# Part of the last zero fill written from GpSimd's DMA queue by 108 rows, in a decode layer with its gradients

## The chip, the cores and the metric

The kernel runs on one core of one Trainium2 chip. The metric is the device time of one execution in microseconds. Before the change it is 814.44 us, the median of 3 runs (814.18 to 814.63).

## The reference

One decode step of a transformer block (layer norm, attention over a sliding window of a key/value cache, a bilinear gated feed-forward part) and its gradients with respect to all inputs and weights:

```
W = min(4096, max(256, Sk // 4))                      # 4096 of Sk = 32768 positions
q = (x @ wq).reshape(B, Sq, Hq, Dh)                   # 16 heads of 256, x has 448 columns
k, v = k_cache[:, :, Sk - W:], v_cache[:, :, Sk - W:] # 8 key/value heads
o = softmax(q k^T / 16) v @ wo
h  = x + A(layernorm(x), k_cache, v_cache, wq, wo)
h2 = h + ((z @ w_gate) * (z @ w_up)) @ w_down,  z = layernorm(h)
outputs: h2, and d/d(x, k_cache, v_cache, wq, wo, w_gate, w_up, w_down) of <h2, grad_out>
```

What matters here: the gradients of the two caches have the full shape (8, 32768, 256) in bf16, and only the last 4096 positions of each head are not zero. The other 28,672 positions of 8 heads and 2 caches, 234.88 MB, are zeros that the kernel has to write. Everything else is about 103 MB of loads and stores.

## The kernel before

Two queues carry the DMAs. SP (in the code `FILL`) issues the two loads of one-row vectors and the zero fills; GpSimd (`IO`) issues all other loads and stores. The DMAs of both run on the same 16 DMA engines of the core.

*The fills.* A tile `zeros` of 128 rows by 8192 bf16 (16 KB a row) is set to zero once on VectorE. For each of 8 heads and for each of the two cache gradients (`out_2` for keys, `out_3` for values) one DMA at line 62 writes the head's zero region: the region is cut into 128 parts of 7 pieces of 16 KB, and row p of `zeros` is written seven times into part p. That makes 16 DMAs of 896 pieces, 14,336 KB each. They are issued at the start, one after the other, as far as SP's queue has room.

*The forward part.* For each head, GpSimd loads windows of the key and value cache (lines 79, of 2 MB each) into slots of the tile `S`; TensorE transposes and multiplies, VectorE and ScalarE empty the results. Loads are issued when a slot comes free.

*The turn.* After the last head the output projection, the feed-forward part and its gradient run with little data: GpSimd issues the second half of `wo` (line 375), `w_gate` (line 376) and `w_up` (line 377), and its next DMA is the second load of `w_down` (line 491), which waits until VectorE has done with the tile `Rt` that held `w_up`.

*The backward part.* For each head a value window is used again (some are loaded again), the gradients of the windows are formed by outer products (line 601), emptied by ScalarE and VectorE (lines 210 and 212), and stored by GpSimd from four staging slots (line 606). Weight gradients are formed on VectorE and stored between them (line 476). GpSimd's issues stand in program order, each behind the waits of those ahead of it.

The order of GpSimd's DMAs is that of the program as scheduled; the completion counters that its DMAs increase are eight, used in turn, so that a DMA that reuses one waits for the DMA eight issues before it.

Of the kernel before, what the change touches and what calls it, by code (L numbers as in the profile page):

```python
# [16 lines left out]
G = 8  # L17
Dh = 256
W = 4096
# [3 lines left out]
Sk = 32768  # L23
# [7 lines left out]
ZW = 8192  # L31
NZ = (Sk - W) * Dh // (128 * ZW)
# [8 lines left out]
def kernel(  # L41
# [4 lines left out]
    FILL = nc.sync  # L46
    IO = nc.gpsimd
# [8 lines left out]
    FILL.dma_start(out=go_bf[:], in_=grad_out.rearrange("a b d -> (a b) d"))  # L56
    zeros = const.tile([128, ZW], bf16)
    V_.memset(zeros[:], 0.0)
    for g in range(G):
        for o in (out_2, out_3):  # L60
            reg = o[0, g, 0:Sk - W, :].rearrange("s d -> (s d)").rearrange("(p n f) -> p n f", p=128, f=ZW)
            FILL.dma_start(out=reg, in_=zeros[:].unsqueeze(1).to_broadcast([128, NZ, ZW]))


    S = const.tile([128, NS, SLOT], bf16)
# [21 lines left out]
    def flat_rows(w):  # L87
        return w.rearrange("a b -> (a b)").rearrange("(p x) -> p x", p=128)
# [251 lines left out]
    wu_sb = Rt[:, 0:NI * HF]  # L340
# [33 lines left out]
                                        op0=ALU.mult, op1=ALU.add, accum_out=d_hh[:, c:c + 1])  # L374
    IO.dma_start(out=woB, in_=wo_v[:, 16:32, :])
    IO.dma_start(out=wg_sb, in_=flat_rows(B_w_gate))
    IO.dma_start(out=wu_sb, in_=flat_rows(B_w_up))


    ao = ps.tile([1, D], f32, tag="tmp", bufs=1)  # L380
# [258 lines left out]
```

## Time and profile before

| | |
|---|---|
| median of 3 runs | 814.44 us |
| span of the profiled execution, first to last instruction | 812.7 us |
| TensorE busy | 495.5 us (61%) |
| VectorE busy | 374.0 us (46%) |
| ScalarE busy | 164.7 us (20%) |
| GpSimd busy, with its issuing of DMAs aside | 40.5 us (5%) |
| read from and written to HBM | 57.28 MB and 280.59 MB, 416 GB/s over the span |
| fills, from issue to landing, median | 148.2 us, 16 times 14,336 KB |
| stores of window gradients, from issue to landing, median | 29.3 us, 16 times 2,048 KB |
| last issue of GpSimd | 769.9 us |

How to read the profile: times are microseconds from the start of the span. The engines' shares say how long each was busy, not what the end waits for. "DMA" in the slices is the mean busy share of the core's 16 DMA engines, a digit of 9 meaning 90% or more. Beside them the profile lists three kinds of DMA queue: those fed by SP in hardware, those fed by GpSimd in software, and the fetches of instructions. The time from issue to landing of a DMA holds the time it stands in its queue behind others.

### The profile page before, as it was taken

The numbers are of one execution on the slowest core, as the hardware profiler recorded it, in microseconds if no ns is written. First come the engines' busy times: TensorE is split into PE (matmuls) and PEld (weight loads), VectorE is DVE, ScalarE is ACT, GpSimd is POOL, SyncE is SP. The second block draws the span as 40 slices with busy tenths as digits, with TensorE's granted clock in tenths as the row PEclk, the third lists the DMA queues.
The fourth block names the chain that finished last, engine by engine and source line by source line (L and its number), as shares of the span: only waits on it lengthen the run. The fifth ranks groups of instructions, "written<-read, shape, count | busy, mean of one in ns | idle before, by whom it ended". The sixth has DMA issues, their size and how long they took to land.

```text
span 812.7 us, 10923 instructions
## 1 busy us (share of the span) xinstructions
PE 495.5 (61%) x4479; PEld 289.6 (36%) x4479; DVE 374.0 (46%) x1149; ACT 164.7 (20%) x261; POOL 40.5 (5%) x75
## 2 busy tenths in 40 slices
PE   3559949999647519035497576099759674554500
PEld 3545636666223405013495432044325331210100
DVE  4128727777445306005671455366455435352500
ACT  0230101222000200001001233044435342332300
POOL 3000000000000001000000100001000001000000
PEclk9959778999678758655556555555555555555555
DMA  8999999999999999999999999999999999999994
GB/s 344 427 426 429 427 433 424 432 424 429 431 422 431 418 429 429 409 430 429 427 427 433 423 410 418 430 428 417 424 406 429 424 418 419 420 427 422 427 427 187
DMA packets 24567, 338.58 MB, mean 417 GB/s; under 512 B 1251, under 2 KB 1317, under 8 KB 4677
## 3 DMA queue, kind: packets, MB, share of 16 engines
q1 hardware_dynamic: 14596, 234.88, 68.4%
q0 software_dynamic: 9920, 103.00, 30.3%
q8 instruction: 35, 0.57, 0.3%
q14 instruction: 16, 0.12, 0.0%
HBM read 57.28 MB, written 280.59 MB: 416 GB/s over the span
## 4 chain that ended last, share of the span: by engine, by line
issue 29%; DMA 16%; PE 11%; DVE 4%; POOL 2%; ACT 1%; POOLq 0%; DVEq 0%
DMA S<-in_A_v_cache_dram 4%; DMA S<-in_A_wo_dram 4%; DMA Rt<-in_A_wq_dram 4%; DMA out_dram<-Mt 3%; PE dq_ps L452 3%; PE MT L322 2%; POOL out_dram L476 1%; DVE Rt L422 1%; POOL out_dram L606 1%; PE dh_ps L159 1%; PE d_ps L601 1%; PE tr L567 1%; PE t L412 1%; PE ao L382 1%; DVE Rt L511 1%
## 5 line engine op out<-in xcount | busy, mean ns | idle before, releaser
L601 PE MATMUL d_ps<-R,Mt 32*128 32x512 bf16 x256 | 124.4, 613 | 92.4 <-DVE S L212 91.6
L322 PE MATMUL MT<-Rt,S 128*128 128x512 bf16 x512 | 145.9, 397 | 30.7 <-DMA S<-in_A_v_cache_dram 29.8
L318 DVE TENSOR_SCALAR Rt<-S,pf 128x256 bf16<-128x256 bf16 x512 | 117.0, 281 | 56.4 <-PE MT L322 49.7
L212 DVE CAST S<-d_ps 128x512 bf16<-128x512 f32 x128 | 86.7, 688 | 55.5 <-ACT S L210 44.0
L210 ACT CAST S<-d_ps 128x512 bf16<-128x512 f32 x128 | 75.0, 586 | 169.8 <-PE d_ps L601 169.8
L601 PEld LDWEIGHTS <-Mt 32*128 32x128 bf16 x256 | 23.3, 114 | 146.1 <-issue 144.7
L567 PE MATMUL tr<-ident_bf,S 128*128 128x128 bf16 x512 | 69.6, 306 | 3.5 <-ACT Mt L210 3.5
L325 PEld LDWEIGHTS <-S 128*128 128x128 bf16 x512 | 49.4, 100 | 60.9 <-issue 9.5
L266 PE MATMUL tr<-ident_bf,S 128*128 128x128 bf16 x512 | 48.6, 253 | 36.4 <-DMA S<-in_A_k_cache_dram 32.0
L567 PEld LDWEIGHTS <-S 128*128 128x128 bf16 x512 | 49.2, 137 | 28.0 <-issue 27.8
L266 PEld LDWEIGHTS <-S 128*128 128x128 bf16 x512 | 38.1, 115 | 34.7 <-DMA S<-in_A_k_cache_dram 32.3
L325 PE MATMUL acc<-pT_all,S 128*128 128x2 bf16 x512 | 48.2, 166 | 0.0
L328 PE MATMUL acc<-pT_all,S 128*128 128x2 bf16 x512 | 47.5, 164 | 0.0
L322 PEld LDWEIGHTS <-S 128*128 128x128 bf16 x512 | 33.5, 98 | 36.7 <-DMA S<-in_A_v_cache_dram 30.7
L210 ACT COPY Rt<-tr 128x1024 bf16<-128x1024 bf16 x32 | 32.4, 1012 | 67.2 <-PE tr L266 66.9
L210 ACT COPY Mt<-tr 128x1024 bf16<-128x1024 bf16 x32 | 32.4, 1014 | 56.6 <-PE tr L567 29.5
L330 ACT COPY Mt<-MT 128x512 f32<-128x512 f32 x8 | 4.7, 585 | 192.3 <-PE MT L322 164.3
L382 PE MATMUL ao<-S,oT_bf 128*1 128x448 bf16 x32 | 9.6, 468 | 45.9 <-DMA S<-in_A_wo_dram 45.9
L212 DVE COPY Rt<-tr 128x1024 bf16<-128x1024 bf16 x32 | 22.0, 688 | 32.7 <-PE tr L266 31.8
L572 PEld LDWEIGHTS <-Mt 128*128 128x128 bf16 x512 | 20.0, 108 | 37.0 <-DVE Mt L212 14.0
L328 PEld LDWEIGHTS <-S 128*128 128x128 bf16 x512 | 30.9, 97 | 0.1
L572 PE MATMUL dp<-doT,Mt 128*128 128x2 bf16 x512 | 22.6, 168 | 12.6 <-DVE Mt L212 10.8
(182 smaller groups left out, 454.5 us busy)
## 6 DMA issues: line engine op xcount, KB each, us to landing
out_dram<-zeros SPq DMA_DIRECT2D x16, 14336.0 KB, 148.2
out_dram<-S POOLq DMA_DIRECT2D x16, 2048.0 KB, 29.3
S<-in_A_v_cache_dram POOLq DMA_DIRECT2D x11, 2048.0 KB, 36.3
S<-in_A_k_cache_dram POOLq DMA_DIRECT2D x8, 2048.0 KB, 29.0
out_dram<-Mt POOLq DMA_DIRECT2D x6, 896.0 KB, 22.2
S<-in_A_wq_dram POOLq DMA_DIRECT2D x1, 3584.0 KB, 14.8
S<-in_A_wo_dram POOLq DMA_DIRECT2D x2, 1792.0 KB, 31.8
out_dram<-Mt POOLq DMA_DIRECT2D x3, 1024.0 KB, 34.0
```

What stands on the lines that cost most here:

```text
L210: S_.copy(out=out, in_=in_)
L212: V_.tensor_copy(out=out, in_=in_)
L266: P_.transpose(tr[:, i, dh, :], Xw[:, 4 * q + i, dh * 128:(dh + 1) * 128], ident_bf[:])
L318: V_.tensor_scalar(out=pk[:, i, h, :], in0=K[:, t, :], scalar1=pf[:, t, h:h + 1], scalar2=None, op0=ALU.mult)
L322: P_.matmul(MT[:, hf, :], lhsT=Vv[:, t, hf * 128:(hf + 1) * 128], rhs=pk[:, i, :, :].rearrange("p h d -> p (h d)"), start=(t == 0), stop=( ...
L325: P_.matmul(acc[:, 2 * hf:2 * hf + 2], lhsT=Vv[:, t, hf * 128:(hf + 1) * 128], rhs=pT_all[:, g, t, :], start=(t == 0 and hf == 0), stop=(t ...
L328: P_.matmul(acc[:, 4 + dk:7 + dk:2], lhsT=K[:, t, dk * 128:(dk + 1) * 128], rhs=pT_all[:, g, t, :], start=False, stop=(t == T - 1), skip_g ...
L382: P_.matmul(ao[:], lhsT=oT_bf[:, b:b + 1], rhs=wo_b(b), start=(b == 0), stop=(b == 31))
L452: P_.matmul(dq_ps[:, 2 * h + dk:2 * h + dk + 1], lhsT=Mt[:, h // 2, hf, c0:c0 + 128], rhs=doT_f[:, 2 * h + hf:2 * h + hf + 1], start=(hf = ...
L567: P_.transpose(tr[:, i, dh, :], Vw[g][:, 4 * q + i, dh * 128:(dh + 1) * 128], ident_bf[:])
L572: P_.matmul(dp[:, 4 * q + i, :], lhsT=xt[:, i, dh, :], rhs=doT[:, 4 * g + dh:4 * g + dh + 3:2], start=(dh == 0), stop=(dh == 1))
L601: P_.matmul(d_ps[:, i, :, :].rearrange("p w d -> p (w d)"), lhsT=rows[32 * k:32 * k + 32, a, :], rhs=R[32 * k:32 * k + 32, :], start=True, ...
```

## The change

Fifteen of the sixteen fills stay as they are. The last one (head 7, `out_3`) is cut at five places. In units of pieces (16 KB) of its 896:

- pieces 0 to 639 are written by SP as before, in one DMA of 128 rows with 5 pieces each;
- the next 614,400 bytes (37.5 pieces) are written by SP in one DMA of 64 rows with one piece of 9,600 bytes each;
- then 14 KB by GpSimd, in one DMA of 7 rows with two pieces of 1 KB each;
- then 26 KB by GpSimd, in one DMA of 13 rows with two pieces of 1 KB each;
- pieces 680 to 895, 216 of them, by GpSimd, in one DMA of 108 rows with two pieces of 16 KB each.

GpSimd issues its three DMAs in the order 7 rows, 108 rows, 13 rows, directly behind its load of `w_up` in the turn and ahead of the second load of `w_down`. All bytes that were written are still written, each once.

```diff
+    def region(o, g):
+        return o[0, g, 0:Sk - W, :].rearrange("s d -> (s d)")
+
+    def fill(eng, flat, p, n, f):
+        eng.dma_start(out=flat.rearrange("(p n f) -> p n f", p=p, f=f), in_=zeros[0:p, 0:f].unsqueeze(1).to_broadcast([p, n, f]))
+
     for g in range(G):
         for o in (out_2, out_3):
-            reg = o[0, g, 0:Sk - W, :].rearrange("s d -> (s d)").rearrange("(p n f) -> p n f", p=128, f=ZW)
-            FILL.dma_start(out=reg, in_=zeros[:].unsqueeze(1).to_broadcast([128, NZ, ZW]))
+            if (g, o) != (G - 1, out_3):
+                fill(FILL, region(o, g), 128, NZ, ZW)
+    last = region(out_3, G - 1)
+    CUT = [0, 640 * ZW, 680 * ZW - 40 * 512, 680 * ZW - 26 * 512, 680 * ZW, NZ * 128 * ZW]
+    fill(FILL, last[CUT[0]:CUT[1]], 128, 5, ZW)
+    fill(FILL, last[CUT[1]:CUT[2]], 64, 1, 4800)
+
+    def fill_rest():
+        fill(IO, last[CUT[2]:CUT[3]], 7, 2, 512)
+        fill(IO, last[CUT[4]:CUT[5]], 108, 2, ZW)
+        fill(IO, last[CUT[3]:CUT[4]], 13, 2, 512)
...
     IO.dma_start(out=wg_sb, in_=flat_rows(B_w_gate))
-    IO.dma_start(out=wu_sb, in_=flat_rows(B_w_up))
+    wu_load = IO.dma_start(out=wu_sb, in_=flat_rows(B_w_up))
+    with tc.issue_after(wu_load.ins):
+        fill_rest()
```

## The prediction

> **What bounds the kernel now.** I read the page's slices and queues first, then the pool engine's timeline around the edit, then the last microseconds by windows, then the single DMA packets.
>
> From the page: the slices, and the DMA queues with packets, megabytes and share of 16 engines.
>
> ```profile
> DMA  8999999999999999999999999999999999999994
> GB/s 344 427 426 429 427 433 424 432 424 429 431 422 431 418 429 429 409 430 429 427 427 433 423 410 418 430 428 417 424 406 429 424 418 419 420 427 422 427 427 187
> DMA packets 24567, 338.58 MB, mean 417 GB/s; under 512 B 1251, under 2 KB 1317, under 8 KB 4677
> ...
> q1 hardware_dynamic: 14596, 234.88, 68.4%
> q0 software_dynamic: 9920, 103.00, 30.3%
> q8 instruction: 35, 0.57, 0.3%
> ```
>
> All 16 DMA engines are busy from the first slice to the last but one, at about 427 GB/s. Compute, the chain of waits included, only decides which bytes go when; the end is when the busiest DMA engine has moved its bytes. q1 is the zero fills that SP issues, q0 everything that GpSimd issues. The change moves bytes from q1 to q0 and adds none.
>
> The last stretch in windows; the last two columns are DMA share and GB/s.
>
> ```profile
> 780.00:790.00 10.00, 0.00 (x0) 0.00 (x0) 0.00 (x0) 0.00 (x0) 0.00 (x0) 0.50 1.02 431
> 790.00:796.00 6.00, 0.00 (x0) 0.00 (x0) 0.00 (x0) 0.00 (x0) 0.00 (x0) 0.50 0.99 421
> 796.00:800.00 4.00, 0.00 (x0) 0.00 (x0) 0.00 (x0) 0.00 (x0) 0.00 (x0) 0.50 0.85 365
> 800.00:803.00 3.00, 0.00 (x0) 0.00 (x0) 0.00 (x0) 0.00 (x0) 0.00 (x0) 0.50 0.37 158
> 803.00:805.00 2.00, 0.00 (x0) 0.00 (x0) 0.00 (x0) 0.00 (x0) 0.00 (x0) 0.50 0.21 90
> 805.00:807.00 2.00, 0.00 (x0) 0.00 (x0) 0.00 (x0) 0.00 (x0) 0.00 (x0) 0.50 0.12 49
> 807.00:809.00 2.00, 0.00 (x0) 0.00 (x0) 0.00 (x0) 0.00 (x0) 0.00 (x0) 0.50 0.06 25
> 809.00:811.10 2.10, 0.00 (x0) 0.00 (x0) 0.00 (x0) 0.00 (x0) 0.00 (x0) 0.50 0.05 23
> ```
>
> No engine computes any more. Shares of 0.21, 0.12 and 0.06 of sixteen are about 3, 2 and 1 engines: a few are late, and the last 4 us belong to one. The trace's packet records name no engine, but a packet starts 3 or 4 ns before the previous one of its engine ends, so engines can be followed. Their ends: twelve from 796.1 to 802.3 us (mean 799.9), then 804.6, 804.7, 806.7 and 811.1. The mean of all sixteen is 801.6: perfect balance would be worth 9.5 us. From 811.1 it is 1.6 us to the span's end (812.7), and 1.7 more to the median of the runs (814.44), so I carry differences at 811.1 over to 814.44.
>
> Why they are late: followed to 450 us, one engine's 16 KB fill pieces take 635 ns on average, the others' 612 to 619. The 35 fetches of q8, about 0.95 us each, go round eight engines in turn; the two that end at 804.6 and 804.7 have one of the last two fetches each. So the late four have different causes, and nothing in the trace says that they are neighbours in the engines' numbering.
>
> The turn, on the pool engine (start, duration, idle before), and the queues between 367 and 395 us.
>
> ```profile
> 320.39 0.53 POOL L376 DMA_DIRECT2D S<-in_B_w_gate_dram  x1 [52.12 <-PE acc L328]
> 321.97 1.17 POOL L375 DMA_DIRECT2D S<-in_A_wo_dram  x1 [1.04 <-PE acc L325]
> 324.32 0.54 POOL L377 DMA_DIRECT2D Rt<-in_B_w_up_dram  x1 [1.19 <-issue]
> 395.07 1.10 POOL L491 DMA_DIRECT2D Rt<-in_B_w_down_dram  x1 [70.21 <-DVE st L196]
> ```
>
> ```profile
> q1 hardware_dynamic: 750, 12.04, 100.5%
> q8 instruction: 1, 0.02, 0.2%
> ```
>
> GpSimd issues nothing for 70 us, and once the w_up load has landed (the view of the DMA issues gives 42.5 us, so 324.3 + 42.5 = 367 us) q0 is empty; the fills alone keep the engines full.
>
> **The change, part by part.**
>
> *Issues.* Three GpSimd DMAs of about 0.53 us behind w_up fall into its 70 us of idling: nothing. If that cover were gone they would delay the w_down load at L491 by 1.6 us, a fifteenth of its 25.8 us to landing. Nothing they wait for is late: the zeros are written at the start, and each later GpSimd DMA that reuses a completion counter waits for one eight issues older, as before. On SP the sixteenth fill becomes two DMAs; a fill lands 63 us or more after its issue begins, so SP's queue does not run dry.
>
> *q0.* 18 pieces alternating with the fills on one engine take 2 x 18 x 0.607 = 21.9 us, from 367 to 389, before the next user at 395. If they take longer, the w_down load is late by the rest; the DMA engines stay full meanwhile, so this alone costs nothing at the end.
>
> *Bytes per engine, the point of it.* A fill gives each engine 896 / 16 = 56 pieces. Now SP gives it 640 / 16 = 40 pieces and 4 of 9,600 bytes, together 42.34 pieces: 13.66 fewer, at 0.607 us 8.3 us less. The 216 pieces come back on q0. Spread evenly they would be 13.5 per engine and nothing would change. 108 rows do not split over 16 engines in whole rows; over 12 they do, 9 rows or 18 pieces each, and 7 + 12 + 13 = 32 brings a cursor round to where it was. Then twelve engines get 10.9 us and four get none. Short rows: two pieces of 1 KB at about 0.045 us and a few counts of 9 ns, 0.15 us. Net: twelve engines +2.75 us, four -8.1 us. No DMA of before has fewer than 16 engines, so which four is not in the trace.
>
> [...]
>
> *Reading rows that belong to others.* Every DMA of before has 128 rows (the one-row vectors aside), and sixteen engines then run side by side at 611 ns for 16 KB. With 9 rows per engine the 108-row DMA has the engines read zeros from rows that other engines' fills are reading at the same time. No row of before shows that. Lower bound: nothing, pieces at 611 ns. Upper bound: pieces of 1,208 ns occur (around 469 us, on most engines, when two pieces of one engine are in flight together), twice 611; if each of the 216 pieces takes that and holds another engine's piece up as long, 2 x 216 x 0.597 = 258 us of engine time, 16.1 us per engine. An engine at 611 ns has no slack to lend, and in a window of 22 us or more nearly all partners are reading; but part of the time the owner of a row is itself reading elsewhere. I take the half, 8 us per engine.
>
> [...]
>
> *Sum.* If the late four are the spared ones: 811.1 - 8.1 + 8 = 811.0 for the last of them, and 802.3 + 2.75 + 8 = 813.1 for the last of the twelve. The loss will not be even; 0.9 us more for that gives 814.0, 2.9 us later than 811.1: 814.44 + 2.9 = **817.3 us**.
>
> **The rivals.**
>
> *No crossing, late ones spared.* The twelve end at 802.3 + 2.75 = 805.1, the four by 803.0: 6.0 us earlier, 808.4 us. If only the last one and the one before it are among the four, 804.7 + 2.75 = 807.5 ends it: 3.6 us earlier, 810.8. For it: the packets' arithmetic above is exact. Against: it needs free reads, and four late engines of different causes as neighbours. From a loss of about 6 us per engine on, it is no gain.
>
> *Wrong four, no crossing.* The engine that ends at 811.1 gets 18 pieces: 811.1 + 2.75, so 817.2. With the crossing as well, 825.2.
>
> *It does not do what it says.* All sixteen engines take part, seven rows each and the last three: fifteen change by 14 - 13.66 pieces, 0.2 us, plus 0.15: 814.8 without crossing. If the engine with 6 pieces is the last one, 806.7 + 0.35 ends it: 810.4.
>
> **How the numbers follow.** About 1.6 us (0.2%) is what can be told from no change. Chances: crossing decides, 0.46; no crossing or little of it and the last engine spared, 0.37; wrong four without crossing, 0.07; sixteen engines, 0.05; a small crossing that cancels the gain, 0.05. Faster: 0.37 and a little from the fourth, 0.38. Same: 0.08. Slower: 0.54. The range goes from 808.0 (all balance gained) to 822.5, which leaves out the full upper bound of the crossing (802.3 + 2.75 + 16.1 = 821.1, so 824.5) and the wrong four with crossing. The likeliest case alone spans 815 to 822.5.
>
> **What would show it.** Pieces of q0 that write zeros between 367 and 390 us: twelve chains of 18 if the split is right. Their duration, and that of the fill pieces beside them: near 611 ns refutes the crossing, 800 to 1,200 proves it, with GB/s of that stretch falling from 431 to about 316 (22 us of work in 30). The last windows: shares falling from 1 to 0 within 3 us mean balance; a lone engine after 811 means the wrong four. The prediction is wrong if the stretch stays at 425 GB/s and the last packet ends by 808.

## The result and the profile after

The changed kernel takes 819.80 us (median of 4 runs, 819.03 to 820.24) beside 814.52 us for the kernel before (4 runs): 5.3 us slower, a ratio of 1.0066 with a 95% interval of 1.0052 to 1.0081. The profiled execution has a span of 818.3 us. The prediction put it at 817.3 us, 2.9 us above the kernel before; the direction was right, the size a little over half of the measured one.

The page of the changed kernel, the same rows as before:

```profile
DMA  8999999999999999999999999999999999999995
GB/s 344 430 424 429 425 430 429 426 428 430 426 426 430 419 425 412 425 426 332 399 430 429 409 423 416 432 421 425 421 410 425 427 416 422 422 424 424 425 427 205
DMA packets 24758, 338.58 MB, mean 414 GB/s; under 512 B 1398, under 2 KB 1464, under 8 KB 4844
...
q1 hardware_dynamic: 14420, 231.30, 67.7%
q0 software_dynamic: 10288, 106.58, 31.3%
```

The bytes are the same, 338.58 MB; 3.58 MB have gone from q1 to q0. The row of busy shares looks as before, all nines. The row of GB/s does not: the 19th slice has 332 and the 20th 399, where before there were 427 and 427. The engines were "busy" in that stretch and moved a fifth less. That is the signature of packets that take longer, not of packets that are missing.

In windows, the last two columns are DMA share and GB/s. First the turn in the kernel before:

```profile
360.00:396.00 36.00, 15.47 (x151) 9.89 (x148) 22.23 (x64) 3.75 (x7) 0.93 (x1) 0.55 1.01 430
```

Then the changed kernel, the turn and the end:

```profile
367.00:390.00 23.00, 8.43 (x120) 4.83 (x119) 17.32 (x40) 3.49 (x6) 0.00 (x0) 0.50 1.00 335
390.00:420.00 30.00, 25.69 (x118) 25.37 (x119) 21.62 (x82) 0.53 (x1) 1.15 (x1) 0.50 1.00 412
...
800.00:803.00 3.00, 0.00 (x0) 0.00 (x0) 0.00 (x0) 0.00 (x0) 0.00 (x0) 0.50 1.05 402
803.00:805.00 2.00, 0.00 (x0) 0.00 (x0) 0.00 (x0) 0.00 (x0) 0.00 (x0) 0.50 0.95 314
805.00:807.00 2.00, 0.00 (x0) 0.00 (x0) 0.00 (x0) 0.00 (x0) 0.00 (x0) 0.50 0.90 258
807.00:809.00 2.00, 0.00 (x0) 0.00 (x0) 0.00 (x0) 0.00 (x0) 0.00 (x0) 0.50 0.61 184
809.00:811.00 2.00, 0.00 (x0) 0.00 (x0) 0.00 (x0) 0.00 (x0) 0.00 (x0) 0.50 0.41 140
811.00:813.00 2.00, 0.00 (x0) 0.00 (x0) 0.00 (x0) 0.00 (x0) 0.00 (x0) 0.50 0.25 100
813.00:815.00 2.00, 0.00 (x0) 0.00 (x0) 0.00 (x0) 0.00 (x0) 0.00 (x0) 0.50 0.09 34
815.00:817.00 2.00, 0.00 (x0) 0.00 (x0) 0.00 (x0) 0.00 (x0) 0.00 (x0) 0.50 0.05 19
```

Two things stand here. In the turn the DMA engines moved 335 GB/s at a share of 1.00. And between 803 and 807 us, while SP's last DMA (64 rows of 9,600 bytes, from 802.0 us on) is written, they are busy at 0.95 and 0.90 and move 314 and 258 GB/s: a second place where they are slow, which the prediction does not have.

GpSimd's issues in the turn (start, duration, idle before):

```profile
323.38 0.54 POOL L392 DMA_DIRECT2D Rt<-in_B_w_up_dram  x1 [1.19 <-issue]
324.00 1.99 POOL L63 DMA_DIRECT2D out_dram<-zeros  x3
392.04 1.15 POOL L508 DMA_DIRECT2D Rt<-in_B_w_down_dram  x1 [66.05 <-DVE st L211]
```

The three added DMAs cost 1.99 us of issuing, and 66 us of idling lie behind them. The w_down load goes out at 392.04 (before: 395.07). The instructions of TensorE, VectorE and ScalarE, and GpSimd's other DMAs, stand in the same order as before, and GpSimd's last issue is at 768.3 us (before: 769.9). So nothing of the loss is a late computation.

The packet records give the rest; followed as in the prediction, from each packet to the next one of its engine:

```
                                    before            after
pieces of 16 KB in the turn, q1     mean 612 ns       mean 810 ns, 54% within 5% of 611, longest 1,785
pieces of 16 KB in the turn, q0     (none)            mean 740 ns, 55% within 5% of 611, longest 1,888
time above 611 ns, all of them      -                 83 us in all, 5.2 us per engine
64 pieces of 9,600 bytes at the end (none)            361 ns alone; nearly half of them 700 to 1,449 ns
ends of the 16 engines              796.1 to 811.1    804.4 to 816.8
mean of the ends                    801.6             809.9
```

The mean end is 8.3 us later at equal bytes, and the last engine ends 5.7 us later.

### The profile page after: what moved, and what is told of

Read it like the earlier page. It is cut to its first block, busy times and chain, and to the rows that moved or that the text cites. A ratio compares the mean times of both kernels' runs of the same rounds, so it can differ in the third digit from the quotient of the medians.

```text
span 818.3 us, 10895 instructions
## 1 busy us (share of the span) xinstructions
PE 493.4 (60%) x4445; PEld 289.5 (35%) x4479; DVE 374.6 (46%) x1149; ACT 164.7 (20%) x261; POOL 42.4 (5%) x78
## 2 busy tenths in 40 slices
DMA packets 24758, 338.58 MB, mean 414 GB/s; under 512 B 1398, under 2 KB 1464, under 8 KB 4844
## 4 chain that ended last, share of the span: by engine, by line
issue 26%; DMA 21%; PE 9%; DVE 4%; POOL 2%; ACT 1%; POOLq 0%; DVEq 0%
DMA out_dram<-S 5%; DMA S<-in_A_v_cache_dram 5%; DMA S<-in_A_wo_dram 4%; DMA Rt<-in_A_wq_dram 4%; DMA out_dram<-Mt 3%; PE d_ps L618 2%; PE MT L337 2%; PE tr L584 2%; POOL out_dram L493 1%; DVE Rt L439 1%; PE t L429 1%; PE ao L399 1%; POOL out_dram L623 1%; DVE Rt L528 1%; DVE S L227 0%
## 5 line engine op out<-in xcount | busy, mean ns | idle before, releaser
L337 PE MATMUL MT<-Rt,S 128*128 128x512 bf16 x478 | 139.9, 398 | 29.5 <-DMA S<-in_A_v_cache_dram 28.9
L584 PE MATMUL tr<-ident_bf,S 128*128 128x128 bf16 x512 | 69.6, 306 | 3.5 <-ACT Mt L225 3.5
L281 PE MATMUL tr<-ident_bf,S 128*128 128x128 bf16 x512 | 50.8, 260 | 33.9 <-DMA S<-in_A_k_cache_dram 28.5
```

The source lines that it names most:

```text
L281: P_.transpose(tr[:, i, dh, :], Xw[:, 4 * q + i, dh * 128:(dh + 1) * 128], ident_bf[:])
L337: P_.matmul(MT[:, hf, :], lhsT=Vv[:, t, hf * 128:(hf + 1) * 128], rhs=pk[:, i, :, :].rearrange("p h d -> p (h d)"), start=(t == 0), stop=( ...
L584: P_.transpose(tr[:, i, dh, :], Vw[g][:, 4 * q + i, dh * 128:(dh + 1) * 128], ident_bf[:])
```

## The experiments

Each edit is shown against the changed kernel. "Mean end" and "last end" are those of the sixteen engines in the profiled execution; in the kernel before they are 801.6 and 811.1. Each ratio is to the kernel before as it ran beside that kernel.

| kernel | median us | ratio to before, 95% interval | GB/s 367 to 390 | mean end | last end |
|---|---|---|---|---|---|
| changed kernel | 819.80 | 1.0066 [1.0052, 1.0081] | 335 | 809.9 | 816.8 |
| e1, 128 rows | 814.14 | 0.9998 [0.9989, 1.0008] | 432 | 802.0 | 811.0 |
| e2, 112 rows | 819.94 | 1.0066 [1.0049, 1.0083] | 342 | 808.0 | 817.3 |
| e3, SP's last DMA with 128 rows | 817.56 | 1.0040 [1.0025, 1.0055] | 343 | 808.2 | 813.9 |
| e6, e3 with the split four engines further | 823.09 | 1.0107 [1.0090, 1.0124] | 336 | 808.2 | 819.5 |
| e4, own rows, first try | 819.59 | 1.0064 [1.0049, 1.0079] | 345 | 811.5 | 815.9 |
| e5, own rows | 815.59 | 1.0008 [0.9997, 1.0020] | 431 | 806.0 | 807.3 |
| e8, e5 with GpSimd's order held | 818.10 | 1.0058 [1.0045, 1.0071] | 430 | 812.9 | 813.0 |
| e9, e8 with 12 pieces | 819.41 | 1.0055 [1.0039, 1.0070] | 428 | 815.1 | 815.1 |
| e10, e5 with every engine's order held | 810.25 | 0.9951 [0.9938, 0.9963] | 426 | 802.7 | 806.6 |
| e11, e10 with 12 pieces | 809.21 | 0.9941 [0.9927, 0.9954] | 427 | 802.0 | 805.7 |

### e1 and e2: the same move with 128 and with 112 rows

Is it the move to the other queue that costs, or the rows that are read? With 128 rows each engine was taken to read the rows that it reads in the fills; with 112 rows every engine gets seven rows, 14 pieces (976 packets of 4 bytes on q0, 61 x 16: all sixteen take part), so that no engine's bytes change, but the rows were taken to be no longer those of its fills.

```diff
-    CUT = [0, 640 * ZW, 680 * ZW - 40 * 512, 680 * ZW - 26 * 512, 680 * ZW, NZ * 128 * ZW]
+    CUT = [0, 640 * ZW, NZ * 128 * ZW]                 # e1
+    CUT = [0, 640 * ZW, 672 * ZW, NZ * 128 * ZW]       # e2
     fill(FILL, last[CUT[0]:CUT[1]], 128, 5, ZW)
-    fill(FILL, last[CUT[1]:CUT[2]], 64, 1, 4800)
+    fill(FILL, last[CUT[1]:CUT[2]], 128, 1, 2048)      # e2 alone
     def fill_rest():
-        fill(IO, last[CUT[2]:CUT[3]], 7, 2, 512)
-        fill(IO, last[CUT[4]:CUT[5]], 108, 2, ZW)
-        fill(IO, last[CUT[3]:CUT[4]], 13, 2, 512)
+        fill(IO, last[CUT[1]:CUT[2]], 128, 2, ZW)      # e1
+        fill(IO, last[CUT[2]:CUT[3]], 112, 2, ZW)      # e2
```

> 256 pieces go to GpSimd in the turn by 128 rows with two pieces each; SP writes the other 640 by 128 rows. Every engine gets what it had before, and no row is read by another engine than before. Crossing theory (engines lose time when they read rows that other engines' fills read): no loss, GB/s between 367 and 390 us stays at 425 to 431, time as before within 1 us (814.5). Rival, that fills from GpSimd's queue in the turn are themselves slow or delay the turn: 335 GB/s there as in the changed kernel, and 818 to 821 us.

> 224 pieces go to GpSimd in the turn by 112 rows with two pieces each, which 16 engines share evenly, seven rows or 14 pieces each; SP writes the rest by 128 rows. No engine gets more or less bytes than before. Crossing theory: the rows do not fit the engines, so GB/s between 367 and 390 us falls to 320 to 360, the engines lose 5 to 7 us each, and the time is 819 to 822 us. Rival, that the changed kernel is slow because of which engines it loads and spares: no difference in bytes, so as before, 814.5 us.

The turn of e1 and then of e2, in windows:

```profile
367.00:390.00 23.00, 9.02 (x122) 5.36 (x122) 16.32 (x39) 3.76 (x7) 0.00 (x0) 0.50 1.01 432
```

```profile
367.00:390.00 23.00, 10.17 (x129) 6.37 (x128) 14.91 (x40) 3.75 (x7) 0.00 (x0) 0.50 1.00 342
```

e1 is the kernel before to within 0.1%: 256 pieces through GpSimd's queue in the turn cost nothing, neither their issue nor their alternation with the fills. e2 gives every engine the same bytes as before, uses all sixteen, has no short rows and no DMA of 64 rows, and is as slow as the changed kernel. What differs between the two, as far as the runs show it, is which rows of the tile are read and by which engine. (In both, a row is written into one strip of 32 KB of the same region, so the places written are an unlikely cause; no run changes them alone.) The pieces of e2 above 611 ns sum to 78 us of engine time, those of e1 to 1.1 us. So the crossing is there, and costs by itself 6.0 us in the mean end (808.0 against 802.0).

### e3 and e7: SP's last DMA with 128 rows

```diff
-    fill(FILL, last[CUT[1]:CUT[2]], 64, 1, 4800)
+    fill(FILL, last[CUT[1]:CUT[2]], 128, 1, 2400)
```

> The changed kernel, with SP's last DMA of 64 rows with 9,600 bytes made one of 128 rows with 4,800 bytes. Crossing theory, second place: its 64 pieces took 361 ns alone and up to 1,450 ns, and GB/s fell to 258 at 805 to 807 us while 0.90 of the DMA engines were busy; with 128 rows this goes, and the time falls by 1 to 2 us, to 818 to 819 us. If the shape of the last DMA does not matter: 819.8 us as the changed kernel.

> The same kernel as e3, run after other kernels that moved the cursor of GpSimd's queue, to see whether it starts where it did. If the cursor is where it was: 817.6 us within 1 us. If it was left elsewhere: 4 us or more later.

The turn and the end of e3:

```profile
367.00:390.00 23.00, 9.02 (x122) 5.36 (x122) 16.23 (x41) 3.75 (x7) 0.00 (x0) 0.50 1.01 343
...
800.00:805.00 5.00, 0.00 (x0) 0.00 (x0) 0.00 (x0) 0.00 (x0) 0.00 (x0) 0.50 0.97 412
805.00:810.00 5.00, 0.00 (x0) 0.00 (x0) 0.00 (x0) 0.00 (x0) 0.00 (x0) 0.50 0.55 232
```

The turn is as slow as in the changed kernel; the end is not: 412 GB/s at a share of 0.97, full rate, where the changed kernel falls to 314 and 258 at shares of 0.95 and 0.90. The same 614,400 bytes in 128 rows instead of 64 are worth 819.80 - 817.56 = 2.2 us, and 1.7 us in the mean end. e7 is the same kernel once more, beside other runs: 817.12 us in its one run, so this does not hang on the occasion, and by its expectation the cursor, the engine with which the next GpSimd DMA of fewer than sixteen engines is taken to begin, starts where it did.

### e6: the split four engines further

Pads of 11 and 9 rows instead of 7 and 13, on top of e3: the four engines that are spared are meant to be the next four.

```diff
-    CUT = [0, 640 * ZW, 680 * ZW - 40 * 512, 680 * ZW - 26 * 512, 680 * ZW, NZ * 128 * ZW]
+    CUT = [0, 640 * ZW, 680 * ZW - 40 * 512, 680 * ZW - 18 * 512, 680 * ZW, NZ * 128 * ZW]
...
-        fill(IO, last[CUT[2]:CUT[3]], 7, 2, 512)
+        fill(IO, last[CUT[2]:CUT[3]], 11, 2, 512)
         fill(IO, last[CUT[4]:CUT[5]], 108, 2, ZW)
-        fill(IO, last[CUT[3]:CUT[4]], 13, 2, 512)
+        fill(IO, last[CUT[3]:CUT[4]], 9, 2, 512)
```

> The changed kernel with SP's last DMA of 128 rows (as e3), with first and last short DMAs of 11 and 9 rows instead of 7 and 13, so that the 108 rows go to other twelve engines and the spared four are shifted by four. Crossing theory with the late four spared by the changed kernel: the same loss in the turn (335 to 350 GB/s), but now the engine that was last gets 18 pieces more instead of none: 6 to 10 us later than e3, 823 to 828 us. Rival, that the changed kernel spared the wrong four: the same as e3 (817.6 us) or earlier.

The end of e6:

```profile
810.00:815.00 5.00, 0.00 (x0) 0.00 (x0) 0.00 (x0) 0.00 (x0) 0.00 (x0) 0.50 0.15 63
815.00:820.00 5.00, 0.00 (x0) 0.00 (x0) 0.00 (x0) 0.00 (x0) 0.00 (x0) 0.50 0.05 21
```

A share of 0.05 from 815 on is one engine, alone: it ends at 819.5, the next at 813.5. The mean end is that of e3, the last end 5.6 us later, the time 823.09 - 817.56 = 5.5 us longer. So the split of the change does spare the engine that ended last, and its place is worth 5.5 us. Whether the other three late ones are spared too, e6 does not show.

### e4 and e5: own rows

If the crossing is the loss, the same split without it should be a gain. Instead of 108 rows by two pieces, each of the twelve engines gets one row 18 times, and a row that is its own in the fills. Which row that is, the profile does not say: the rows of the edit (28 for the first of the twelve, 64, 68 .. 92 for the next eight, 0, 4, 8 for the last three) are the author's assumption. So is the cursor: each of these DMAs is taken to begin behind the last engine of the one before it, the pads of 7 rows at 0, so that the twelve engines are 7 to 15 and 0 to 2. No record names an engine, but the trace of the changed kernel agrees with an order of this kind: in its DMA of 7 rows seven engines have a packet of 2,048 bytes and nine have one of 8 (362.5 to 365.5 us), the nine are all among the twelve of the DMA of 108 rows behind it, and its four idle engines are all among the seven. Whether the rows fit is for the durations of the pieces to show.

```diff
+    def fill_own(lo, hi, r0, p, n):
+        IO.dma_start(out=last[lo:hi].rearrange("(p n f) -> p n f", p=p, f=ZW),
+                     in_=zeros[r0:r0 + 4 * (p - 1) + 1:4, 0:ZW].unsqueeze(1).to_broadcast([p, n, ZW]))
...
-        fill(IO, last[CUT[4]:CUT[5]], 108, 2, ZW)
+        fill_own(a3, a4, 28, 1, 17)        # e4: row 28, then rows 64, 68 .. 92, then rows 0, 4, 8
+        fill_own(a4, a5, 64, 8, 18)
+        fill_own(a5, a6, 0, 3, 18)
```

> [...] SP's last DMA has 128 rows. Crossing theory: no loss in the turn (425 GB/s), the balance remains, 6 us less than before: 808 to 810 us. [...] Rival, that the four spared engines are the wrong ones: 817 us with 425 GB/s in the turn.

e4 missed its expectation for two reasons of its own. Its one-row DMA of 17 pieces was not done by one engine but spread over nine, two pieces on each of eight and the last on a ninth. (The packets of 4 bytes that GpSimd's DMAs leave on idle engines, counted further below, fit this: 15 belong to it, two on each of seven idle engines and one on the ninth.) Eight engines then read row 28 at once: between 367 and 377 us thirteen packets of q0 took 2.0 to 4.7 us each instead of 0.61, and two of the fills beside them 2.8 and 4.8 us. The stretch from 390 to 420 us moved 392 GB/s, so the later DMAs crossed too, presumably because the cursor was not where the edit had it. And the order of the work had moved, as in e5 below: the last two stores were issued at 799.45 and 800.17 us. So its time says nothing on own rows. But those packets are the crossing at its purest: eight readers of one row, each slowed up to 7.7 times.

e5 has no such DMA: 2 rows (28 and 64), 7 rows (68, 72 .. 92) and 3 rows (0, 4, 8), each 18 times, between pads of 7 and 13; SP's last DMA has 128 rows of 4,800 bytes.

```diff
+    def fill_own(lo, hi, r0, step, p):
+        IO.dma_start(out=last[lo:hi].rearrange("(p n f) -> p n f", p=p, f=ZW),
+                     in_=zeros[r0:r0 + step * (p - 1) + 1:step, 0:ZW].unsqueeze(1).to_broadcast([p, 18, ZW]))
...
-        fill(IO, last[CUT[4]:CUT[5]], 108, 2, ZW)
+        fill_own(a3, a4, 28, 36, 2)
+        fill_own(a4, a5, 68, 4, 7)
+        fill_own(a5, a6, 0, 4, 3)
```

> The twelve engines and the four spared ones as in the changed kernel, 18 pieces each, but every engine reads one row of zeros that its own fills read, with two rows 36 apart for the first two engines, seven rows four apart for the next seven and three rows four apart for the last three (the kernel e4 tried this with one row of 17 pieces, which was spread over nine engines and turned the rest away from its rows). SP's last DMA has 128 rows of 4,800 bytes. Crossing theory: 425 to 431 GB/s in the turn instead of 335 to 345, twelve engines end 2.75 us later than before, the spared ones 8 us earlier, and the time is 808 to 810 us, faster than both kernels. If the rows do not fit: slower than the changed kernel without the 64-row DMA, 818 us or more. Rival, wrong four engines spared: 425 GB/s, but 817 us.

The turn and the end of e5:

```profile
367.00:390.00 23.00, 8.43 (x120) 4.84 (x119) 17.32 (x40) 3.49 (x6) 0.00 (x0) 0.50 1.02 431
...
790.00:800.00 10.00, 3.17 (x8) 0.58 (x5) 3.02 (x5) 2.35 (x4) 1.07 (x2) 0.50 0.80 335
```

The first half of the expectation held exactly: 431 GB/s in the turn, and the 163 recorded zero pieces of q0 that begin between 365 and 395 us took 611 ns on average and 611 at most. The crossing is gone, so each of the twelve rows of the edit went to an engine that reads it without loss. How the other 116 rows lie on the engines, no run shows. The second half, the gain, did not come: the median is that of the kernel before. The profiled execution was the fastest of ten, 811.3 us; the other nine, 814.7 to 816.4, left no trace. The second line shows what held even that one up: between 790 and 800 us TensorE, VectorE and ScalarE still compute, which they did not before, and the DMA engines are only 0.80 busy. GpSimd issued its last two stores at 794.8 and 795.5 us instead of 769.2 and 769.9; the last fill packet ended at 796.2 us, so the DMA engines had too little to do while they waited for these stores. In this kernel GpSimd's DMAs and the instructions of the compute engines stand in another order than before. The scheduler, which sets the order when the kernel is built, was given five DMAs in place of three; why it then chose this order was not looked into.

### e8 and e9: GpSimd's order held

e8 is e5 with GpSimd's DMAs held in the order of the kernel before, by edges that set an order and wait for nothing; e9 is the same with 12 pieces per engine. Of the edit, the lines that hold the order:

```diff
+    for a, b in zip(line, line[1:]):     # GpSimd's DMAs, as they stood before
+        tc.add_manual_dep(b, a.name, mybir.DependencyInfo(mybir.DependencyClass.NoSync, mybir.DependencyReason.DATA), reason="order")
```

> As e5 (each of the twelve engines reads only its own rows, 18 pieces), and GpSimd's other DMAs are held in the order that they have in the kernel before, by edges that set an order and wait for nothing. Theory (the crossing was the whole loss, and e5 was held back only by its last store, issued at 795.5 us instead of 769.9): pieces of q0 at 611 ns, the last store issued by about 785, the ends at 811.1 - 8.1 = 803.0 for the last of the spared and 802.3 + 2.75 = 805.1 for the last of the twelve, 6.0 us earlier than before: 808.4 (807 to 811). Rival A (the placeholder packets on unused engines make the three DMAs run one after the other to about 410 us, the w_down load and all that hangs on it come 15 us later, and the stores end the kernel again): 812 to 816, with all sixteen engines ending together. Rival B (sparing the late engines is worth nothing by itself): 814 to 815 with the ends spread as before.

> As e8_order18 with 12 pieces instead of 18 on each of the twelve engines, and 128 rows of 14,016 bytes as SP's last DMA. Theory: the spared engines give up 12 x 0.75 x 0.607 = 5.5 us and the twelve take 1.8 us, so 811.1 - 5.5 = 805.6 ends it, 5.5 us earlier than before: 809.0 (807.5 to 811). The three data DMAs take 2 x 12 x 0.61 = 15 us each and end near 411 - 14 = 397 us, so Rival A (late w_down load) would cost a third less here than in e8: 810 to 814, and this one would be the faster of the two. Rival B: 814 to 815.

Both were slower than e5, against the theory as it stood. GpSimd's issues behind the w_down load in e8:

```profile
393.96 1.14 POOL L54 DMA_DIRECT2D Rt<-in_B_w_down_dram  x1 [66.32 <-DVE st L235]
432.65 0.57 POOL L54 DMA_DIRECT2D out_dram<-Mt  x1 [37.55 <-DVE kd L496]
493.13 0.54 POOL L54 DMA_DIRECT2D out_dram<-Mt  x1 [59.90 <-DVE Mt L516]
...
802.54 0.53 POOL L54 DMA_DIRECT2D out_dram<-S  x1 [0.19 <-issue]
```

The second weight-gradient store waits 59.90 us for VectorE and goes out at 493.13 (448.49 in the kernel before); GpSimd then stays late to the end, 802.54 against 769.89 (804.73 in e9). The queue was held in order, but VectorE, ScalarE and TensorE were still scheduled otherwise and prepared the stores in another sequence. Holding one queue of several made it worse than leaving all to the scheduler. All sixteen engines end together (812.9), which is the picture of a late last store. Whether Rival A, the placeholders, had a part was open after this.

### e10 and e11: every engine's order held

The same, with every instruction of TensorE, VectorE, ScalarE and GpSimd in the order of the kernel before, the five DMAs of the split behind `w_up`. Of the edit, the lines that hold the order:

```diff
+    for e, text in ORDER.items():        # the order of each engine before, written out
...
+        for a, b in zip(line, line[1:]):
+            tc.add_manual_dep(b, a.name, mybir.DependencyInfo(mybir.DependencyClass.NoSync, mybir.DependencyReason.DATA), reason="order")
```

> As e8 (own rows, 18 pieces on each of twelve engines), but every instruction of TensorE, VectorE, ScalarE and GpSimd is held in the order that it has in the kernel before; in e8 only GpSimd's was, and the other engines' later order still made the last store 32.7 us late (802.5 against 769.9). Theory (the crossing was the loss, and the order alone kept e5 and e8 from the gain): last store issued by about 785 us, pieces of q0 at 611 ns, the last of the spared engines at 811.1 - 8.1 = 803.0 and the last of the twelve at 802.3 + 2.75 = 805.1, so 6.0 us earlier than before: 808.4 (807 to 811). Rival A (the placeholder packets make the w_down load land some 15 us later, and the compute behind it, not the order, makes the stores late): last store after 790, 811 to 816, all engines ending together. Rival B (sparing the late engines is worth nothing by itself): 814 to 815 with ends spread as before.

> As e10_full18 with 12 pieces instead of 18 on each of the twelve engines. Theory: the spared give up 12 x 0.75 x 0.607 = 5.5 us and the twelve take 1.8 us: 811.1 - 5.5 = 805.6 ends it, 809.0 (807.5 to 811). The data DMAs end some 14 us earlier than in e10, so by Rival A this one would be the faster of the two (809 to 813) and by the theory the slower by half a microsecond. Rival B: 814 to 815.

GpSimd's issues in e10:

```profile
395.05 1.14 POOL L531 DMA_DIRECT2D Rt<-in_B_w_down_dram  x1 [66.81 <-DVE st L232]
433.74 0.57 POOL L516 DMA_DIRECT2D out_dram<-Mt  x1 [37.55 <-DVE kd L495]
448.41 0.54 POOL L516 DMA_DIRECT2D out_dram<-Mt  x1 [14.10 <-DVE Mt L515]
...
767.59 0.53 POOL L646 DMA_DIRECT2D out_dram<-S  x1 [0.19 <-issue]
```

The end of e11 in windows:

```profile
790.00:796.00 6.00, 0.00 (x0) 0.00 (x0) 0.00 (x0) 0.00 (x0) 0.00 (x0) 0.50 1.00 427
796.00:800.00 4.00, 0.00 (x0) 0.00 (x0) 0.00 (x0) 0.00 (x0) 0.00 (x0) 0.50 0.95 402
800.00:803.00 3.00, 0.00 (x0) 0.00 (x0) 0.00 (x0) 0.00 (x0) 0.00 (x0) 0.50 0.54 231
803.00:805.00 2.00, 0.00 (x0) 0.00 (x0) 0.00 (x0) 0.00 (x0) 0.00 (x0) 0.50 0.18 77
805.00:807.00 2.00, 0.00 (x0) 0.00 (x0) 0.00 (x0) 0.00 (x0) 0.00 (x0) 0.50 0.02 7
```

The stores go out when they did before (448.41 and 767.59), and the balance arrives: the last engine ends at 805.7 in e11, where the expectation worked out 805.6, and nobody is alone after 807. e11 takes 809.21 us, 0.6% less than the kernel before, and beats both kernels; e10 takes 810.25. The w_down load landed 38.1 us after its issue in e10, 25.8 before, and the store behind it still went out at 433.74 (433.79 before): the delay that Rival A counted is there and is hidden. Against the kernel before as it ran beside them, 814.22 us, e10 gains 4.0 of the 6.0 us that were worked out for it, and e11 5.0 of 5.5. e11 was 1.0 us faster than e10 where the theory had it half a microsecond slower, but the two intervals overlap, so which is faster is not settled. The last engine of e10 ended at 806.6 instead of 805.1. Of these 1.5 us, 0.7 stand in the mean end too (802.7 against 802.0 in e11); what they are was not followed up.

## Why the prediction came out as it did

**The bound.** Right: the end is the busiest DMA engine. Every kernel whose last store is issued by 773 us ends as its engines' chains do, 2.6 to 3.7 us before the measured median.

**Issues, q0.** Right in effect. The three issues took 1.99 us instead of 1.6 and were hidden. The pieces on q0 took longer than the 21.9 us of the sum: the last ended at 394.2, not at 389. The w_down load went out at 392.04 and was not held up (25.2 us to landing, 25.8 before). e1 shows the price of queue and issue together: none.

**Bytes per engine, and which four.** Right, and better founded than the prediction could have it. Packets of 4 bytes on q0 number 960 before, sixteen for each of 60 GpSimd DMAs, and 1,080 after: 63 x 16 = 1,008 and 72 more, which is 4 idle engines x 18 pieces; of 8 bytes there are none before and 12 after, 16 - 7 and 16 - 13. (e2 has 976 of 4 bytes, 61 x 16: all sixteen engines.) So the DMA of 108 rows used twelve engines. For the round of 7 + 12 + 13 = 32 the packets speak less surely, since they crowd in the turn: in the likeliest following the three engines with 8 bytes in the DMA of 13 rows are the three that have 2,048 bytes in the one of 7 rows and pieces in the one of 108, and every engine takes part in two of the three DMAs. (The other 60 DMAs of GpSimd used all sixteen engines; SP's two one-row loads are one packet of 896 bytes each.) That the engine that ended last is among the four, e6 shows with 5.5 us. The prediction held "four late engines of different causes as neighbours" against this. For the second-latest, which ended at 806.7, e10 and e11 speak: with its share it would end at 806.7 + 2.75 = 809.4 and 806.7 + 1.8 = 808.5, an estimate, and no engine there ends after 806.6 and 805.7. For the other two no run settles it. The rivals of the wrong four and of sixteen engines fall.

**Reading rows that belong to others.** Right as a mechanism; e2 has it alone, e5, e10 and e11 have all but it. The size taken, 8 us per engine, was too high for it: e3, without the 64-row DMA, has a mean end 6.2 us behind e1's, and e2 one of 6.0. The expected form was wrong as well. "800 to 1,200" ns were forecast for the pieces; more than half stayed at 611 ns and the others took up to three times that. So engines seem to meet for a piece and part again, and the prediction's "nearly all partners are reading" counted too many meetings; that is a reading of these durations, not shown by a run. Nor do the runs tell whether two engines must be on the same row, or whether rows hang together in groups.

**The unevenness.** 0.9 us was allowed for it. In e3 the last engine ends at 813.9, and the forecast was 814.0 for just this case; but it came from a mean loss 1.8 us smaller (6.2 for 8) and a spread 1.7 us wider (802.3 + 2.75 + 6.2 = 811.3, and 2.6 more to 813.9, where 0.9 was allowed). That the two errors cancel is luck.

**The term that was missing.** The step that failed is the one on SP's DMAs. The prediction says that "the sixteenth fill becomes two DMAs" and counts "4 of 9,600 bytes" per engine at the full rate. It didn't ask which rows these are, 64 of 128. Nearly half of the 64 packets (28) took 700 ns and more where one alone takes 361, and 16 KB pieces of the fills beside them up to 1,405. The question that the prediction puts to the 108 rows, whether other engines' fills are reading the same rows at the same time, stands for these 64 too, and was put to the one DMA and not to the other; the trace has 258 GB/s at a share of 0.90. That the number of rows decides and not the size of the packets, e3 and e11 show: of 128 rows with 4,800 bytes none took more than 199 ns, of 128 with 14,016 bytes none more than 536, and the fill pieces beside them in e3 none more than 624. e3 measures it: 2.2 us of the 2.5 between 817.3 and 819.8. Without it the time is 817.56.

**The rival that was nearly as likely.** "No crossing, late ones spared" at 808.4 needs "free reads". e10 and e11 are that case, built: 810.25 and 809.21. The balance was worth two thirds of the sum in e10 and nine tenths in e11. Against e10, which moves the same pieces, the changed kernel is 9.6 us slower: 2.2 for the 64-row DMA and 7.3 for the crossing in the turn (817.56 in e3 against 810.25). So the crossing took back more than the balance gave.

## What to carry to other kernels

Where the DMA engines were the bound here, a split that evens out their bytes paid only when each engine read a row of its own (810.25 and 809.21 us in e10 and e11, 819.80 with the 108 rows): look at GB/s against busy share in the stretch, because the share hid the loss (1.00 at 335 GB/s, 1.01 at 426 in e10). Check each DMA of an edit for this, the small one at the end too. And an edit that a scheduler sees differently moves work on engines that it doesn't touch: compare the order on all of them before blaming the hardware, and hold the order on all of them or on none.

## What the runs showed of the hardware that was not expected

A GpSimd DMA that used fewer than sixteen engines put packets on the others as well. The counts of 4-byte packets fit one on each idle engine for each piece of a used one: 72 in the changed kernel, and in e10 1,688 = 65 x 16 + 18 x (14 + 9 + 13), in e11 1,472 = 65 x 16 + 12 x 36. Each seems to take its turn with a 16 KB piece of the fills: in the changed kernel those of one idle engine start 613 ns apart from 366.3 to 368.1 us, with a fill piece of 611 ns between, and in e10 two engines' pieces come from 366 us on, the next seven engines' from about 376, the last three engines' run until 411, which is 18 x 0.61 = 11 us of waiting for each DMA ahead. Three such DMAs in a row took 45 us for 18 pieces per engine; the one of 108 rows took 30 with its crossing. In DMA time this cost little: the mean end of e10 is 802.7, that of e1 802.0.

A one-row GpSimd DMA of 17 pieces was spread over nine engines (e4), though 108, 13, 7, 3 and 2 rows went to 12, 13, 7, 3 and 2 engines; and eight engines that read one row of the tile took up to 4.7 us for 16 KB, 7.7 times 0.61.
